# Attention scores computed once per head in 64x32 array tiles, with an expert loop that turns each block's rows at its own start

## The chip, the cores and the metric

The kernel runs on one core of a Trainium2 chip. A core has TensorE (matrix products, written PE in profiles, with its weight loads as PEld), VectorE (DVE), ScalarE (ACT), GpSimd (POOL) and SyncE (SP), which here only issues transfers. Each engine works through its own instructions in order and waits for others through semaphores. The metric is the device time of one execution in microseconds (us); all data are 32-bit floats.

## The reference

There are B = 8 batches of H = 8 heads. Each head has 512 rows of x and 32 rows of state, of width 64. The first half is an attention in both directions, the second a mixture of 8 experts in which a token either takes the expert of its own largest logit or keeps that of the token before.

```python
scores = scale * x @ state.T              # (512, 32) per head
a = softmax(scores, over the 32)          # x reads from the state
xread = a @ state
scores2 = scale * state @ x.T             # (32, 512): the same numbers, turned
a2 = softmax(scores2, over the 512)       # the state reads from x
sread = a2 @ x
x = concat([xread, sread], rows)          # per batch 544 tokens of 8*64 = 512

logits = x @ w_gate                       # 8 per token
local_gate = sigmoid(x @ w_local)
e = argmax(logits) if first token or local_gate < 0.5 else expert of the token before
out = softmax(logits)[e] * (relu(x @ w1[e]) @ w2[e])     # 512 -> 1024 -> 512
```

## The kernel before

The program has three stages, one after another: `attention` (L90), `Routing.route` (L282) and `experts` (L395). In all of them a scheduler decides the order in which each engine gets its instructions, from the order of the code and from the dependencies; on the engine the order is then fixed.

**Attention** goes through the 8 batches. The heads of a batch are held as two groups of four (g), each group as two 128-partition slices (k) of two heads. `std` (L105 to L111) holds the state of each head spread with zeros, so that a product over 128 partitions keeps heads apart. `weights(b, g)` (L134) makes the scores twice: `s2` (L139) with the state rows on the partitions and 512 tokens along the row, and `s1` (L145) with tokens on the partitions. From s2 comes the softmax over tokens, `e2` (L149 to L162), and from s1 the one over the 32 state rows, `e1` (L156 to L167; the last multiplication is on GpSimd). `turned` (L170) turns both with TensorE against an identity, e2 at L174 and e1 at L179, and copies them out of PSUM with ScalarE (L176) and VectorE (L181). `read(b)` (L184) makes the state's reading of x (L189), and for each of four chunks of 128 tokens the values (L202, 256 columns for each group) and, with the same weights, the logits (L205, 9 columns: eight experts and the local gate). For the latter, `sw` (state times gate weights, L117 to L125) is made once ahead of the loop. The values leave PSUM at L208, the state's rows are turned at L215 and their logits made at L218. Then the softmax of the logits (L223 to L233) is appended to each row, and rows go to DRAM (L234, L235) as 520 numbers: 512 values and 8 probabilities. The loop (L240) runs `turned` of batch b, the scores of b+1 and `read` of b.

**Routing** finds each token's expert, sorts tokens into blocks of 128 that share an expert, and writes for each block the tokens to gather (`gidx`), the places to scatter to (`sidx`), the expert (`bei`, `ohb`) and the number of blocks in use (`nbi`, L339). 4352 tokens fill between 34 and 41 blocks.

**Experts** runs over the blocks. `gather(k)` (L407) fetches 128 rows by an indirect transfer of GpSimd into one of four buffers. `load(k)` (L413) reads the expert's number into a register of SyncE and loads its two weight matrices, 2 MB each, into one of two buffers each. `turn(k)` (L423) turns the rows with four TensorE transposes (L427), copies them out with VectorE (L429), and picks the probability `p` of the block's expert (L430, L431). `block(k)` (L438) does the first product in two halves (L447) with the relu on ScalarE (L449), then the second product (L458), the scaling by p on VectorE (`y`, L460) and the scatter by GpSimd (L461). Between the two products of block k stand `load(k + 1)`, `turn(k + 1)` and `gather(k + 3)` (L451 to L455). The first 34 blocks run always, the last 7 each under a condition that holds only while blocks are left:

```python
    n = nc.values_load(nbi[0:1, 0:1], min_val=NJ, max_val=NBLK, ...)
    for k in range(NJ):
        block(k)
    with ExitStack() as held:
        for k in range(NJ, NBLK):
            held.enter_context(tc.If(n > k))
            block(k)
```

PSUM is one pool of 8 banks (`bank`, L64) for all stages.

Of the kernel before, what the change touches and what calls it, by code (L numbers as in the profile page):

```python
# [17 lines left out]
P = 128  # L18
# [12 lines left out]
XW = D + E  # L31
# [7 lines left out]
def kernel(  # L39
# [18 lines left out]

    nc = tc.nc
    keep = ctx.enter_context(tc.tile_pool(name="keep", bufs=1))  # L60
    ps = ctx.enter_context(tc.tile_pool(name="ps", bufs=8, space=PSUM))
    dram = ctx.enter_context(tc.tile_pool(name="dram", bufs=1, space=DRAM))

    def bank(parts=P):  # L64
        return ps.tile([parts, 512], F32, tag="ps", name="ps")
# [8 lines left out]
    nbi = keep.tile([1, 1], I32, name="nbi")  # L74
# [7 lines left out]
    route = Routing(ctx, tc, bank, ident)  # L82
    with ExitStack() as phase:
        attention(phase, tc, bank, xn, xt, st, stt, ident, wg, lt, mx, rows)
    route.route(lt, mx, gidx, sidx, ohb, bei, nbi)
    with ExitStack() as phase:
        experts(phase, tc, bank, w1, w2, ident, rows, gidx, sidx, ohb, bei, nbi, out)


def attention(ctx, tc, bank, xn, xt, st, stt, ident, wg, lt, mx, rows):  # L90
# [3 lines left out]
    wk = ctx.enter_context(tc.tile_pool(name="wk", bufs=4))  # L94
    tp = ctx.enter_context(tc.tile_pool(name="tp", bufs=4))
    rp = ctx.enter_context(tc.tile_pool(name="rp", bufs=2))
    sm = ctx.enter_context(tc.tile_pool(name="sm", bufs=4))


    stc = once.tile([P, B, G, DH], F32, name="stc")  # L100
    nc.scalar.dma_start(out=stc.rearrange("p b g d -> p (b g d)"), in_=st)
    sttc = once.tile([P, B, KT, N], F32, name="sttc")
    nc.sync.dma_start(out=sttc.rearrange("p b k n -> p (b k n)"), in_=stt)
    sd = once.tile([P, B, G, GD], F32, name="sd")
    std = once.tile([P, B, KT, P], F32, name="std")  # L105
    nc.vector.memset(std, 0.0)
    nc.gpsimd.memset(sd, 0.0)
    for m in range(2):
        for u in range(2):
            r, c = slice(64 * u, 64 * u + 64), slice(64 * m + 32 * u, 64 * m + 32 * u + 32)  # L110
            nc.vector.tensor_copy(std[r, :, m::2, c], sttc[r, :, m::2, :])  # L111
    for j in range(4):
        r = slice(32 * j, 32 * j + 32)
        nc.scalar.copy(sd[r, :, :, 64 * j:64 * j + 64], stc[r])


    wps = bank()  # L117
    for b in range(B):
        for g in range(G):
            i = (b * G + g) * (E + 1)  # L120
            for k in (2 * g, 2 * g + 1):
                nc.tensor.matmul(wps[:, i:i + E + 1], lhsT=std[:, b, k, :], rhs=wg[:, k, :],  # L122
                                 start=(k == 2 * g), stop=(k == 2 * g + 1))
    sw = once.tile([P, B, G, E + 1], F32, name="sw")
    nc.scalar.copy(sw.rearrange("p b g e -> p (b g e)"), wps[:, :B * G * (E + 1)])  # L125
# [8 lines left out]
    def weights(b, g, x_t):  # L134


        s2 = bank()
        for k in (2 * g, 2 * g + 1):
            nc.tensor.matmul(s2, lhsT=std[:, b, k, :], rhs=x_t[:, k, :],  # L139
                             start=(k == 2 * g), stop=(k == 2 * g + 1))  # L140

        s1 = bank()
        for c in range(SC):
            for k in (2 * g, 2 * g + 1):
                nc.tensor.matmul(s1[:, c * P:c * P + P], lhsT=x_t[:, k, c * P:c * P + P],  # L145
                                 rhs=std[:, b, k, :], start=(k == 2 * g), stop=(k == 2 * g + 1))

        nb = sm.tile([P, 1], F32, name="nb")
        nc.vector.tensor_reduce(nb, s2, axis=AX, op=Alu.max)  # L149
        nc.vector.tensor_scalar(nb, nb, -SCALE, None, Alu.mult)  # L150
        e2 = wk.tile([P, S], F32, name="e2")
        z2 = sm.tile([P, 1], F32, name="z2")
        nc.scalar.activation(e2, s2, Act.Exp, bias=nb, scale=SCALE, accum_out=z2)
        m1 = sm.tile([P, SC * 4, 1], F32, name="m1")
        s1v = s1.rearrange("p (a n) -> p a n", n=N)
        nc.vector.tensor_reduce(m1.rearrange("p a o -> p (a o)"), s1v, axis=AX, op=Alu.max)  # L156
        e1 = wk.tile([P, SC * 4, N], F32, name="e1")
        nc.vector.tensor_tensor(e1, s1v, m1.to_broadcast([P, SC * 4, N]), op=Alu.subtract)
        nc.scalar.activation(e1, e1, Act.Exp, scale=SCALE)
        nc.vector.tensor_scalar(z2, z2, 1e-9, None, Alu.add)  # L160
        nc.vector.reciprocal(z2, z2)  # L161
        nc.vector.tensor_scalar(e2, e2, z2, None, Alu.mult)  # L162
        z1 = sm.tile([P, SC * 4, 1], F32, name="z1")
        nc.vector.tensor_reduce(z1.rearrange("p a o -> p (a o)"), e1, axis=AX, op=Alu.add)
        nc.vector.tensor_scalar(z1, z1, 1e-9, None, Alu.add)
        nc.vector.reciprocal(z1, z1)
        nc.gpsimd.tensor_tensor(e1, e1, z1.to_broadcast([P, SC * 4, N]), op=Alu.mult)  # L167
        return e1.rearrange("p a n -> p (a n)"), e2

    def turned(e1, e2):  # L170

        t2 = bank()
        for c in range(SC):
            nc.tensor.transpose(t2[:, c * P:c * P + P], e2[:, c * P:c * P + P], ident)  # L174
        e = tp.tile([P, SC, P], F32, name="e")
        nc.scalar.copy(e.rearrange("p c n -> p (c n)"), t2)  # L176
        t1 = bank()
        for c in range(SC):
# [324 lines left out]
```

## Time and profile before

| what | value |
|---|---|
| time, median of 3 runs (lowest to highest) | 784.79 us (783.58 to 785.57) |
| the profiled execution's own time | 784.79 us |
| its span, first to last instruction | 783.0 us |
| TensorE busy | 739.7 us (94%) |
| VectorE / ScalarE / GpSimd busy | 185.4 / 107.5 / 100.6 us |
| mean granted TensorE clock | 0.962 |
| moved by DMA | 211.03 MB, mean 270 GB/s |
| attention, to the last product L218 | 178.0 us |
| routing, to the first L447 | 178.0 to 221.2 us |
| experts, to the last y | 221.2 to 772.6 us |
| from there to the end of the span | 10.4 us |

A profile shows one execution. A group of instructions is shown as line, engine, operation, the tiles written and read, shapes and a count, then busy time in us, the mean duration of one in ns, and the idle time of that engine just before with what ended it. The chain of waits follows the last instruction back to what released it, step by step. A matmul's recorded end is a modelled one, so durations of neighbouring matmuls overlap; starts are what can be subtracted. A product of 32-bit floats is recorded as two matmuls, each with its own weight load; a transpose as one. Idle time of an engine that nobody waits for costs nothing.

### The profile page before, as it was taken

How to read it: one execution, taken by the hardware profiler on the slowest of the kernel's cores; microseconds unless marked ns; L12 is line 12 of the kernel's file. 1: busy time of each engine (PE TensorE's matmuls, PEld its weight loads, DVE VectorE, ACT ScalarE, POOL GpSimd, SP SyncE). 2: the span in 40 equal slices, each digit the busy share in tenths (PEclk: the TensorE clock that was granted, in tenths of full speed). 3: DMA queues.
4: the chain of work that ended last, by engine and by line, in shares of the span. 5: the costliest groups of instructions: out<-in, count | busy, mean ns of one | idle time of the engine just before them, and what ended most of it. 6: DMA issues, size and time to landing. Idle time of an engine off the chain costs nothing.

```text
span 783.0 us, 10576 instructions
## 1 busy us (share of the span) xinstructions
PE 739.7 (94%) x4410; PEld 568.0 (73%) x4410; DVE 185.4 (24%) x517; ACT 107.5 (14%) x194; POOL 100.6 (13%) x107
## 2 busy tenths in 40 slices
PE   6799999992879999999999999999999999999994
PEld 6588888891867867767767768778678677677682
DVE  3455555537611011101101111110110111011010
ACT  0433333330000000100100000000001001000000
POOL 2111111110031111111111111111111111111120
PEclk9899999996579999999999999999999999999997
DMA  8134553112948888898888888888888989888881
GB/s 368 62 108 166 186 189 128 59 59 75 412 125 321 343 322 317 332 338 319 325 344 307 319 338 333 315 327 338 311 318 340 328 316 336 334 295 311 333 319 63
DMA packets 24946, 211.03 MB, mean 270 GB/s; under 512 B 3456, under 2 KB 3456, under 8 KB 12864
## 3 DMA queue, kind: packets, MB, share of 16 engines
q1 hardware_dynamic: 13824, 180.90, 62.5%
q0 software_dynamic: 6320, 19.84, 6.5%
q10 hardware_dynamic: 4752, 9.58, 3.3%
q8 instruction: 37, 0.61, 0.3%
q14 instruction: 13, 0.11, 0.0%
HBM read 192.34 MB, written 19.01 MB: 270 GB/s over the span
## 4 chain that ended last, share of the span: by engine, by line
PE 92%; DVE 3%; DMA 2%; issue 1%; POOL 0%; SPq 0%; POOLq 0%; DVEq 0%
PE ps L447 34%; PE ps L458 32%; PE ps L139 4%; PE ps L202 4%; PE ps L145 4%; PE ps L189 4%; PE ps L388 2%; PE ps L427 2%; PE ps L122 2%; PE ps L205 1%; DMA out_dram<-y,sidx 1%; PE ps L179 1%; PE ps L174 1%; DMA sttc<-in_stt_dram 1%; PE ps L215 0%
## 5 line engine op out<-in xcount | busy, mean ns | idle before, releaser
L447 PEld LDWEIGHTS ps<-x_t,a 128*128 128x128 f32 x2432 | 279.5, 193 | 18.9 <-issue 17.7
L447 PE MATMUL ps<-x_t,a 128*128 128x128 f32 x2432 | 279.8, 276 | 0.8 <-DVE x_t L429 0.8
L458 PE MATMUL ps<-c,h 128*128 128x512 f32 x608 | 267.2, 592 | 0.0
L458 PEld LDWEIGHTS ps<-c,h 128*128 128x128 f32 x608 | 112.6, 190 | 127.2 <-issue 127.2
L449 ACT ACTIVATE h<-ps 128x512 f32<-128x512 f32 x76 | 45.4, 597 | 541.6 <-PE ps L447 541.6
L429 DVE COPY x_t<-ps 128x512 f32<-128x512 f32 x39 | 27.0, 692 | 246.6 <-PE ps L427 246.6
L460 DVE TENSOR_SCALAR y<-ps,p 128x512 f32<-128x512 f32 x38 | 28.5, 751 | 234.8 <-PE ps L458 234.8
L461 POOL DMA_INDIRECT out_dram<-y,sidx x38 | 38.4, 1011 | 289.5 <-DVE p L431 263.9
L409 POOL DMA_INDIRECT xg<-rows,gidx x41 | 40.2, 980 | 242.6 <-PE ps L427 188.4
L145 PEld LDWEIGHTS ps<-std,x_t 128*128 128x128 f32 x256 | 31.4, 193 | 8.5 <-issue 8.5
L202 PE MATMUL ps<-sd,a 128*128 128x256 f32 x128 | 35.3, 398 | 0.0
L167 POOL TENSOR_TENSOR e<-e,z 128x512 f32<-128x512 f32 x16 | 16.8, 1048 | 141.3 <-DVE z L161 108.9
L139 PE MATMUL ps<-x_t,std 128*128 128x512 f32 x64 | 33.4, 649 | 0.0
L145 PE MATMUL ps<-std,x_t 128*128 128x128 f32 x256 | 31.2, 275 | 0.0
L189 PE MATMUL ps<-e,x_n 128*128 128x64 f32 x256 | 29.5, 273 | 0.0
L189 PEld LDWEIGHTS ps<-e,x_n 128*128 128x128 f32 x256 | 29.2, 192 | 0.0
L427 PE MATMUL ps<-ident,xg 128*128 128x128 f32 x156 | 23.9, 277 | 4.1 <-DMA xg<-rows,gidx 4.1
L388 PE MATMUL ps<-bc,pc 128*128 128x41 f32 x80 | 17.3, 415 | 9.9 <-DVE bc L383 9.9
L388 PEld LDWEIGHTS ps<-bc,pc 128*128 128x128 f32 x80 | 17.1, 332 | 10.8 <-issue 10.8
L208 ACT COPY xr<-ps 128x512 f32<-128x512 f32 x32 | 18.8, 586 | 36.6 <-PE ps L202 36.6
L202 PEld LDWEIGHTS ps<-sd,a 128*128 128x128 f32 x128 | 21.9, 191 | 1.6
L427 PEld LDWEIGHTS ps<-ident,xg 128*128 128x128 f32 x156 | 18.6, 143 | 4.3 <-issue 4.3
(125 smaller groups left out, 326.4 us busy)
## 6 DMA issues: line engine op xcount, KB each, us to landing
a<-in_w_dram SPq DMA_DIRECT2D x39, 2048.0 KB, 8.4
c<-in_w_dram SPq DMA_DIRECT2D x39, 2048.0 KB
rows<-xr ACTq DMA_DIRECT2D x8, 1040.0 KB, 4.4
x_t<-in_xt_dram SPq DMA_DIRECT2D x8, 1024.0 KB, 8.7
x_n<-in_xn_dram SPq DMA_DIRECT2D x8, 1024.0 KB, 5.1
xg<-rows,gidx POOLq DMA_INDIRECT x41, 7.9
out_dram<-y,sidx POOLq DMA_INDIRECT x38, 6.9
rows<-xs ACTq DMA_DIRECT2D x8, 65.0 KB, 4.0
```

The lines of the kernel that those rows point to most:

```text
L139: nc.tensor.matmul(s2, lhsT=std[:, b, k, :], rhs=x_t[:, k, :], start=(k == 2 * g), stop=(k == 2 * g + 1))
L145: nc.tensor.matmul(s1[:, c * P:c * P + P], lhsT=x_t[:, k, c * P:c * P + P], rhs=std[:, b, k, :], start=(k == 2 * g), stop=(k == 2 * g + 1))
L189: nc.tensor.matmul(rps[:, k, :], lhsT=x_n[:, c, 2 * k:2 * k + 2, :].rearrange("p h d -> p (h d)"), rhs=e_t[k // 2][:, c, 64 * (k % 2):64 * ...
L202: nc.tensor.matmul(v[:, g * GD:g * GD + GD], lhsT=a_t[g][:, c * P:c * P + P], rhs=sd[:, b, g, :], start=True, stop=True)
L388: nc.tensor.matmul(who, lhsT=pc, rhs=bc[:, c], start=(c == 0), stop=(c == COLS - 1))
L409: nc.gpsimd.indirect_dma_start(out=xg, out_offset=None, in_=rows[:, :], in_offset=bass.IndirectOffsetOnAxis(ap=gidx[:, k:k + 1], axis=0))
L427: nc.tensor.transpose(tps[:, j * P:j * P + P], xg[:, j * P:j * P + P], ident)
L447: nc.tensor.matmul(hps[:, i * P:i * P + P], lhsT=a[:, j, m * P:m * P + P], rhs=x_t[:, j, :], start=(j == 0), stop=(j == KT - 1))
L449: nc.scalar.activation(h[:, half * 4:half * 4 + 4, :].rearrange("p m t -> p (m t)"), hps, Act.Relu)
L458: nc.tensor.matmul(yps, lhsT=h[:, m, :], rhs=c[:, m, :], start=(m == 0), stop=(m == FK - 1))
L460: nc.vector.tensor_scalar(y, yps, p, None, Alu.mult)
L461: nc.gpsimd.indirect_dma_start(out=out, out_offset=bass.IndirectOffsetOnAxis(ap=sidx[:, k:k + 1], axis=0), in_=y, in_offset=None, bounds_c ...
```

## The change

The attention is written anew, and the expert loop has another form.

Scores are made once. `sttc`, the state with two heads on the partitions (64 each), is used as it is: for each of the four slices k and two halves u, one product over 64 partitions gives 32 rows, so that the eight products of a batch address eight different 64x32 tiles of the array. They fill a tile of two PSUM banks, `s`. The softmax over tokens works on s as before (e2). For the one over the state's rows, VectorE turns s in 32x32 squares into `e1`; the maximum, the difference (now GpSimd), the exponential, the sum and the quotient follow, and a second 32x32 transpose gives `a`, which then needs no turn on TensorE. The operations on e1 cover both groups, 1024 elements in a row. `gates` puts the state times the gate weights beside the spread state in `sd`, so that one value product of 265 columns gives values and a part of the logits; the parts of the two groups are added (L206). Rows in DRAM have 530 numbers. PSUM is split: two banks in a pool for attention, two for s, four for values; eight for routing and experts, which share a pool opened later. Work buffers of attention have two copies in place of four.

In the experts, buffers come from pools: two copies of the weights, three of the gathered rows. Block k begins with its load, the gather of k+2, p, the four transposes and their copy, and then has its two products, y and the scatter. The conditions and `nbi` are gone: all 41 blocks run. The order of the rows of w1 is changed ahead of the launch to fit the new order of heads.

The core of the diff:

```diff
-XW = D + E
+VW = GD + E + 1
+XW = G * VW
...
+    def scores(b, x_t):
+        s = sps.tile([P, G, S], F32, name="s")
+        for k in range(KT):
+            for u in range(G):
+                r = slice(64 * u, 64 * u + 64)
+                nc.tensor.matmul(s[32 * k:32 * k + 32, u, :], lhsT=sttc[r, b, k, :], rhs=x_t[r, k, :],
+                                 start=True, stop=True)
+        return s
+
+    def gates():
+        for u in range(G):
+            w = bank()
+            r = slice(64 * u, 64 * u + 64)
+            for b in range(B):
+                for k in range(KT):
+                    nc.tensor.matmul(w[32 * k:32 * k + 32, b * (E + 1):(b + 1) * (E + 1)],
+                                     lhsT=sttc[r, b, k, :], rhs=wg[r, k, :], start=True, stop=True)
+            nc.vector.tensor_copy(sd[:, :, u, GD:], w[:, :B * (E + 1)].rearrange("p (b e) -> p b e", b=B))
...
-        nc.vector.tensor_tensor(e1, s1v, m1.to_broadcast([P, SC * 4, N]), op=Alu.subtract)
-        nc.scalar.activation(e1, e1, Act.Exp, scale=SCALE)
+        e1 = wk.tile([P, G * SC * 4, N], F32, name="e1")
+        e1f = e1.rearrange("p a n -> p (a n)")
+        nc.vector.transpose(e1f, s.rearrange("p g s -> p (g s)"))
...
+        nc.vector.tensor_reduce(m1.rearrange("p a o -> p (a o)"), e1, axis=AX, op=Alu.max)
+        nc.gpsimd.tensor_tensor(e1, e1, m1.to_broadcast([P, G * SC * 4, N]), op=Alu.subtract)
+        nc.scalar.activation(e1f, e1f, Act.Exp, scale=SCALE)
...
-        nc.gpsimd.tensor_tensor(e1, e1, z1.to_broadcast([P, SC * 4, N]), op=Alu.mult)
+        nc.gpsimd.tensor_tensor(e1, e1, z1.to_broadcast([P, G * SC * 4, N]), op=Alu.mult)
+        a = tp.tile([P, G, S], F32, name="a")
+        nc.vector.transpose(a.rearrange("p g s -> p (g s)"), e1f)
...
-        t1 = bank()
-        for c in range(SC):
-            nc.tensor.transpose(t1[:, c * P:c * P + P], e1[:, c * P:c * P + P], ident)
-        a = tp.tile([P, S], F32, name="a")
-        nc.vector.tensor_copy(a, t1)
...
         for c in range(SC):
-            v = bank()
-            for g in range(G):
-                nc.tensor.matmul(v[:, g * GD:g * GD + GD], lhsT=a_t[g][:, c * P:c * P + P],
-                                 rhs=sd[:, b, g, :], start=True, stop=True)
-            for g in range(G):
-                nc.tensor.matmul(lps[:, c * (E + 1):(c + 1) * (E + 1)],
-                                 lhsT=a_t[g][:, c * P:c * P + P], rhs=sw[:, b, g, :],
-                                 start=(g == 0), stop=(g == G - 1))
-            nc.scalar.copy(xr[:, c, :D], v)
+            v = vps.tile([P, G, 512], F32, name="v")
+            for u in range(G):
+                nc.tensor.matmul(v[:, u, :VW], lhsT=a[:, u, c * P:c * P + P], rhs=sd[:, b, u, :],
+                                 start=True, stop=True)
+            nc.scalar.copy(xr[:, c], v[:, :, :VW])
+        nc.vector.tensor_tensor(lt[:, :SC, b, :], xr[:, :, 0, GD:], xr[:, :, 1, GD:], op=Alu.add)
...
     for b in range(B):
-        at = [turned(*s) for s in soft.pop(b)]
+        e = turned(soft[1])
+        a = soft[0]
...
         if b + 1 < B:
-            soft[b + 1] = [weights(b + 1, g, xs_[b + 1][0]) for g in range(G)]
+            soft = softmaxes(scores(b + 1, xs_[b + 1][0]))
...
-    def turn(k, xg):
+    xgs = {k: gather(k) for k in range(2)}
+    for k in range(NBLK):
+        a, c = load(k)
+        if k + 2 < NBLK:
+            xgs[k + 2] = gather(k + 2)
+        xg = xgs.pop(k)
+        own = gp.tile([P, E], F32, name="own")
+        nc.vector.tensor_tensor(own, xg[:, GD:GD + E], ohb[:, k], op=Alu.mult)
+        p = gp.tile([P, 1], F32, name="p")
+        nc.vector.tensor_reduce(p, own, axis=AX, op=Alu.add)
         tps = bank()
         for j in range(KT):
...
+            nc.tensor.transpose(tps[:, j * P:j * P + P], xg[:, at:at + P], ident)
+        x_t = hp.tile([P, KT, P], F32, name="x_t")
         nc.vector.tensor_copy(x_t.rearrange("p k t -> p (k t)"), tps)
...
-        if k + 1 < NBLK:
-            ws[k + 1] = load(k + 1)
-            ready[k + 1] = turn(k + 1, xgs.pop(k + 1))
-        if k + 3 < NBLK:
-            xgs[k + 3] = gather(k + 3)
         yps = bank()
...
-    for k in range(NJ):
-        block(k)
-    with ExitStack() as held:
-        for k in range(NJ, NBLK):
-            held.enter_context(tc.If(n > k))
-            block(k)
```

In the changed file the score products are L131, the gate products L141, the 32x32 transposes L153 and L173, the turns of e2 L181, the value products L203, the state's rows L212 and L215; in the experts own is L425, p L427, the transposes L431, their copy L433, the first product L440, the second L445, y L447 and the scatter L448.

## The prediction

> **What bounds the kernel now.** I read the stages first, because the page's mean over the span hides that the program is three different programs. The view of busy time by stage (columns: engine busy us with the number of instructions; the granted TensorE clock; DMA share and rate) gives:
>
> ```profile
> core 0: us, PE busy (x) PEld busy (x) DVE busy (x) ACT busy (x) POOL busy (x), PEclk, DMA share, GB/s
> 64.90:168.50 103.60, 103.60 (x756) 90.00 (x754) 57.97 (x185) 39.94 (x79) 12.59 (x12) 1.00 0.36 127
> 178.00:221.00 43.00, 22.25 (x98) 19.91 (x98) 28.70 (x94) 0.48 (x2) 4.04 (x5) 0.54 0.61 236
> 221.00:772.60 551.60, 551.36 (x3192) 405.61 (x3192) 66.31 (x152) 45.38 (x76) 73.52 (x74) 1.00 0.86 317
> ```
>
> The reader sees TensorE busy without a hole in attention (103.60 of 103.60 us) and in the experts (551.36 of 551.60), and neither in the routing stage between (22.25 of 43.00), which is a chain of small VectorE steps and 40 short products. So a TensorE microsecond removed from attention, or added to the experts, moves the end one for one until another engine becomes late.
>
> The costs of attention are in the groups by form (each product in the code is two recorded matmuls: 32 products at L139, 64 records). A record's mean ns includes its modelled tail, so I take start-to-start times from the timeline where I can:
>
> ```profile
> L139 PE MATMUL ps<-x_t,std 128*128 128x512 f32 x64 | 33.4, 649 | 0.0
> L145 PE MATMUL ps<-std,x_t 128*128 128x128 f32 x256 | 31.2, 275 | 0.0
> L179 PE MATMUL ps<-ident,e 128*128 128x128 f32 x64 | 10.2, 285 | 2.1 <-POOL e L167 2.1
> L205 PE MATMUL ps<-sw,a 128*128 128x9 f32 x128 | 16.3, 236 | 0.0
> L149 DVE TENSOR_REDUCE nb<-ps 128x1 f32<-128x512 f32 x16 | 11.1, 691 | 24.2 <-PE ps L139 24.2
> L167 POOL TENSOR_TENSOR e<-e,z 128x512 f32<-128x512 f32 x16 | 16.8, 1048 | 141.3 <-DVE z L161 108.9 <-PE ps L202 16.4 <-DVE z L166 16.0
> ```
>
> The handover between two expert blocks is in the timeline. Columns: start, duration, engine, line:
>
> ```profile
> 432.78 0.60 PE L427 MATMUL ps<-ident,xg 128*128 128x128 f32 x4
> ...
> 433.21 7.03 PE L458 MATMUL ps<-c,h 128*128 128x512 f32 x16
> 433.41 0.69 DVE L429 COPY x_t<-ps 128x512 f32<-128x512 f32 x1 [6.43 <-PE ps L427]
> ...
> 440.08 6.19 PE L447 MATMUL ps<-x_t,a 128*128 128x128 f32 x54
> 440.28 0.33 SPq L419 DMA_DIRECT2D c<-in_w_dram  x1
> 440.29 0.75 DVE L460 TENSOR_SCALAR y<-ps,p 128x512 f32<-128x512 f32 x1 [6.18 <-PE ps L458]
> ```
>
> The turning of the next block (L427, 0.43 us from its start to the next stream's) stands between the two products of this block, its copy (L429) lies under L458, and L447 of the next block follows L458 at once. Period 14.45 us: 7.15 for L447, 0.43, 6.87 for L458. And the program runs fewer blocks than it holds:
>
> ```profile
> L409 POOL DMA_INDIRECT xg<-rows,gidx x41 | 40.2, 980 | 242.6 <-PE ps L427 188.4 <-DVE gone L391 51.8 <-issue 1.8
> L461 POOL DMA_INDIRECT out_dram<-y,sidx x38 | 38.4, 1011 | 289.5 <-DVE p L431 263.9 <-DVE own L430 13.5 <-DVEq L469 12.2
> ```
>
> 41 gathers but 38 scatters: with this data the conditions (L471) end the loop after 38 of 41 blocks. From the first L447 at 221.23 to the last y at 772.63 are 551.4 us = 38 x 14.45 + 2.3 (a first block at a low clock).
>
> [...] L158, 512 elements, shows 691 ns[...]; so 1024 elements are estimated at 1.22 us. [...] the trace's clock is 1.00 in the experts, so I keep full clock there.
>
> **The change, part by part.** The profiled execution took 784.79 us, span 783.0, and is also the median of the three runs; sums are made against it. It divides into attention to 178.0, routing to 221.2 (43.2), experts 551.4 and a tail of 10.4.
>
> *Expert handover.* In the changed program's order TensorE has L431 (four transposes) right before L440 of the same block, after L445 of the block before. VectorE has y of the block before (L447 there) and right behind it the copy x_t (L433). Let T0 be when the array comes free. Transposes are done by T0+0.43. From the timeline, y starts at T0+0.21 (440.29 against 440.08) and lasts 0.75; back-to-back VectorE instructions start about 0.08 before the former's recorded end (758.18+0.75 against 758.85), so x_t runs from T0+0.88 to T0+1.57; TensorE starts 0.05 later (as at 221.23, behind the copy that ended at 221.18). That is T0+1.62, and 0.10 for a weight load that is no longer hidden: 1.72 where it was 0.43. Period 7.15+6.87+1.72 = 15.74, +1.29. Ends: 1.55 (load hidden, copy overlapping more) and 1.90 (the whole 0.19 us load and slower restarts). Nothing covers it: the array has no other work in its order. Below zero is excluded because the copy stands ahead of the first product in the data flow.
>
> *Three more blocks.* No condition is left, so 41 blocks run; the last three scatter nothing but load weights and multiply. From first L440 to last y: 40 x 15.74 + 14.02 + 2.3 = 645.9, against 551.4: **+94.5** (three blocks about 47, the handovers about 47). The removed conditions and the block count give nothing back: the period is 14.45 before and after block 34. Weight loads keep two buffers and the same releases; 4.2 MB per 15.74 us is a lower rate than now. Of the moved steps: VectorE has own(k+3) ahead of y(k), and it waits for gather k+3, so y and x_t queue behind that gather. It is issued about 1 us into block k and landings here are at most 9.0 us, some 5 us early: cost 0. Without that cover each late microsecond would cost one per block. On POOL gather k+4 stands ahead of scatter k, both at the block's start, 1 us each; y has two buffers and a scatter lands in 6.9: 0.
>
> *Attention on TensorE.* Gone per batch (period 18.42): L139 3.44, L145 3.57, the e1 transposes L179 0.86, L205 1.40 (4 x 0.35): 9.3. Kept: e2 transposes 0.86, L189 3.52, the value products 0.96 per chunk times 265/256 for their 9 extra columns, x 4 = 3.96, L215 and L218 0.88: 9.22. New: 8 score products, each two records of 512 columns at 0.43. Bounds: all tiles at once 0.9[...], one after another 16 x 0.43 = 6.9. I take 9 x 0.43 = 3.9: the second record of a product needs the same tile as the first[...]. So TensorE has 13.1 per batch (10.1 to 16.1).
>
> *Attention on the others, per batch.* VectorE: five passes over 1024 elements (two maxima, one sum, two 32x32 transposes) 6.1; two e2 scalings 1.0; small softmax steps 0.9; rt 0.58; logits 0.36; routing statistics 1.3: 10.2, against 10.3 now (57.97 in 5.63 batches). POOL: two 1024-element operations, 2 x 2.1. ACT about 7.2. So TensorE still leads; a transpose of fp32 at a quarter of the estimated rate would add 7.3 and make VectorE the bound at 17.5. The chain from scores to a (1.22+0.15+1.22+1.22+2.1+1.06+1.22+0.44+2.1+1.22 = 12.0) is hidden in steady state, since scores stand up to two batches ahead of their value products. It shows once, at the start.
>
> *Attention's end.* The gate products: 64, so 128 records; with 32-column weights L218 takes 0.044 each warm, at twice that cold: 5.6 to 11.3, say 8.5, from 5.5 (the state's landing) to 14. First scores to 19. The chain with 1.5 of queueing: first value product at 32.5. Left on TensorE: 8 x (3.96+0.88) + 7 x (0.86+3.52) + 6 x 3.9 = 92.8. With 5 us for waits: **130, against 178: -48**. At the ends: all tiles at once, then VectorE leads: 32 + 7.5 x 10.2 + 4 = 113; in series 32.5 + 110.8 + 9 = 152.
>
> *Routing, tail.* The same instructions but one; 43.4, since the last lt now follows an ACT copy. Tail 10.
>
> Sum: 130 + 43.4 + 645.9 + 10 = 829.3, against 783.0: +46, so **831** for the 784.8.
>
> **Rivals.** *(a) Scores in series or a slow transpose:* the tiles don't overlap. For: two records per product[...]. Attention ends at 152: 853. This is also the case where the change doesn't do what it says. *(b) Attention better:* scores fully side by side, VectorE leads at 10.2: ends at 113, 814. *(c) Handover hidden:* the expert stage keeps 14.45 because TensorE gets its x_t without idling; then 41 x 14.45 + 2.3 = 594.8 is only +43, and attention's -48 leaves 780, faster. It decides once the handover is below about 0.57 (40 x (h-0.43) + 43 = 48). For it: VectorE is busy only 66 of 551 us. Against: the order puts y's 0.75 and the copy's 0.69 in series with TensorE. *(d) The gather ahead of y lands late:* 2 us a block, 910; landings of 9.0 at most speak against it.
>
> **How the numbers follow.** Main case 62% (range 822 to 842); (a) 17%; (b) 15%; (c) 4%; (d) 2%. The range for 8 in 10 takes (a) and (b) in and leaves out their far parts, with 40 x 0.18 = 7 for the handover's bounds partly inside: 812 to 853. About 0.3% is what a measurement of this kernel can tell from no change. Slower 0.95; (c) gives most of faster 0.04; between 0.01.
>
> **What would show it.** 41 scatters; block starts 15.7 apart; TensorE idle about 1.3 a block, ended by the x_t copy; x_t directly behind y. In attention, score records spanning about 3.9 per batch, a period near 13, transposes near 1.2 us, the routing stage starting near 130. Wrong if transposes take several us, if score records stand one behind another, or if own's wait for a gather ends the idle time before y.

## The result, and the profile after

The changed kernel takes 835.23 us (median of 4 runs, 834.05 to 836.63), the kernel before 784.18 in the same comparison (4 runs). The ratio is 1.065, with a 95% interval of 1.0626 to 1.0673: slower by 6.5%. The profiled execution took 836.63 us, its span is 834.8.

The view of busy time by stage, for the changed kernel (29 us is where its first value product starts, 136 where its last one ends, 179.9 where its first expert product starts; columns as before):

```profile
core 0: us, PE busy (x) PEld busy (x) DVE busy (x) ACT busy (x) POOL busy (x), PEclk, DMA share, GB/s
29.00:128.50 99.50, 86.81 (x544) 62.94 (x545) 68.55 (x152) 44.91 (x88) 25.95 (x20) 0.89 0.45 164
128.50:136.00 7.50, 7.50 (x55) 6.51 (x53) 1.64 (x8) 1.79 (x4) 0.00 (x0) 0.92 0.42 155
136.00:179.80 43.80, 22.34 (x99) 19.93 (x98) 28.77 (x94) 0.84 (x2) 3.52 (x4) 0.55 0.60 234
179.80:825.30 645.50, 605.09 (x3440) 436.39 (x3440) 63.50 (x162) 48.97 (x82) 77.26 (x78) 1.00 0.77 284
```

In the experts TensorE was busy in 551.36 of 551.60 us; now it is in 605.09 of 645.50, so 40 us of holes are new. They hold 41 blocks instead of 38. In attention, TensorE was busy without a hole at clock 1.00; now it has 12.7 us of holes in 99.5 us (and none in the 7.5 after them), and the mean clock is 0.89. The routing stage is what it was.

The bill by stage, of the two profiled executions: attention ends at 136.0 instead of 178.0 (-42.0), routing takes 43.9 instead of 43.2 (+0.7), the experts from first product to last y take 645.4 instead of 551.4 (+94.0), the tail 9.5 instead of 10.4 (-0.9). The sum is +51.8, which is the difference of the spans, 834.8 and 783.0.

The groups by form show the new operations and the block count (out<-in, shape, count; busy us, mean ns; idle time before, with its releasers):

```profile
L440 PE MATMUL ps<-x_t,a 128*128 128x128 f32 x2624 | 306.0, 278 | 41.0 <-DVE x_t L433 40.2 <-issue 0.8
L448 POOL DMA_INDIRECT out_dram<-y,sidx x41 | 41.7, 1016 | 69.2 <-DVE y L447 58.0 <-issue 11.3
L131 PE MATMUL s<-x_t,sttc 64*32 64x512 f32 x128 | 20.6, 715 | 9.2 <-ACT e L157 7.2 <-DMA x_t<-in_xt_dram 2.0
L173 DVE STREAM_TRANSPOSE a<-e 128x1024 f32<-128x1024 f32 x8 | 9.9, 1244 | 6.9 <-POOL e L171 6.9
L153 DVE STREAM_TRANSPOSE e<-s 128x1024 f32<-128x1024 f32 x8 | 9.9, 1238 | 0.0
L224 DVE TENSOR_TENSOR pr<-lt,mx 128x40 f32<-128x40 f32 x8 | 7.6, 952 | 0.2
L163 DVE TENSOR_SCALAR z<-z 128x2 f32<-128x2 f32 x8 | 4.0, 494 | 1.3 <-ACT e L157 1.3
L141 PE MATMUL ps<-wg,sttc 64*32 64x9 f32 x128 | 1.8, 199 | 4.3 <-DMA sttc<-in_stt_dram 4.3
```

L440 names the cause of the expert holes: 40.2 us of idle time ended by the copy x_t, 1.00 us for each of 40 handovers. L448 counts 41 scatters where before had 38. A 32x32 transpose of 1024 elements takes 1.24 us, from PSUM (L153) and from SBUF (L173) alike. L224 is the surprise: an operation on 40 elements with a mean of 952 ns. The same step (L226 there) was 200 ns in the kernel before.

One handover, in the timeline of the changed kernel (start, duration, engine, line):

```profile
431.97 0.60 PE L431 MATMUL ps<-ident,xg 128*128 128x128 f32 x4
...
432.17 0.75 DVE L447 TENSOR_SCALAR y<-ps,p 128x512 f32<-128x512 f32 x1 [6.79 <-PE ps L445]
432.84 0.68 DVE L433 COPY x_t<-ps 128x512 f32<-128x512 f32 x1
...
433.57 7.41 PE L440 MATMUL ps<-x_t,a 128*128 128x128 f32 x64 [1.00 <-DVE x_t L433]
...
440.80 0.17 DVE L425 TENSOR_TENSOR own<-xg,ohb 128x8 f32<-128x8 f32 x1 [7.22 <-DMA xg<-rows,gidx]
...
440.82 5.75 PE L445 MATMUL ps<-c,h 128*128 128x512 f32 x13
```

Transposes at 431.97; y occupies VectorE first, from 432.17; the copy comes behind it, at 432.84; the first product starts at 433.57, 1.60 us after the transposes. From there to L445 are 7.25 us, 0.10 more than the 7.15 of before: the first weight load starts together with the first product, where before it lay 0.43 us ahead, under L458. 1.60 + 7.25 + 6.87 = 15.72 is the period; it was 14.45.

### What attention waits for

In three places, holes of TensorE in attention are followed by a stretch at half its clock. TensorE's timeline of the changed kernel at the first of them:

```profile
49.93 0.66 PE L181 MATMUL ps<-ident,e 128*128 128x128 f32 x4
53.94 6.47 PE L190 MATMUL ps<-e,x_n 128*128 128x64 f32 x32 [3.35 <-ACT e L182]
60.20 5.23 PE L203 MATMUL v<-sd,a 128*128 128x265 f32 x12
```

and the windows around it (the number after the busy times is the granted clock):

```profile
core 0: us, PE busy (x) PEld busy (x) DVE busy (x) ACT busy (x) POOL busy (x), PEclk, DMA share, GB/s
52.00:56.00 4.00, 2.06 (x13) 2.06 (x13) 3.11 (x9) 2.16 (x6) 1.91 (x1) 0.83 0.58 236
56.00:60.00 4.00, 4.00 (x21) 4.00 (x20) 1.78 (x5) 0.00 (x0) 1.91 (x1) 0.50 0.00 0
60.00:64.00 4.00, 4.00 (x11) 3.15 (x12) 1.76 (x8) 1.21 (x2) 0.00 (x0) 0.50 0.61 205
```

There are 3.35 us of idle time, then 10.2 us at 0.50 (54.7 to 64.9): L190 takes 6.47 us for the 32 records that take 3.78 at full clock (at 100.91 in the same trace), and the 12 records of L203 5.23 where late_dve, below, has 2.97. So 5 us are lost behind a stall of 3.35. The clock is also 0.50 from 78.6 to 85.4, around the end of the gap that ends at 79.9, and from 122.9 to 129.8, after several gaps from 119 on. Smaller holes, 0.73 us ahead of 29.02 and 0.88 ahead of 36.47, leave it at 1.00. Which length of idle time brings the half clock is not shown here: it came behind a gap of 3.35 us, within one of 4.05, and, in the section below on what was not expected, behind one of 0.92.

Two waits make up most of the 12.7 us: 4.1 us for the copies of the turned e2 (L182; 3.35 of them up to 53.94) and 4.8 us for the transposes of e1 (L173; 4.05 of them up to 79.91).

What made TensorE wait at 50? The second of two ScalarE copies (L182). ScalarE's timeline, same kernel:

```profile
49.03 0.59 ACT L182 COPY e<-ps 128x512 f32<-128x512 f32 x1 [1.27 <-PE ps L181]
53.18 0.24 ACT L225 ACTIVATE pr<-pr 128x40 f32<-128x40 f32 x1 [3.56 <-DVE pr L224]
53.32 0.57 ACT L182 COPY e<-ps 128x512 f32<-128x512 f32 x1
```

The exponential of the logits (L225, 40 elements, of the batch before) stands in ScalarE's order between the two copies, and waits 3.56 us for VectorE's L224. VectorE has meanwhile:

```profile
50.09 1.22 DVE L148 TENSOR_REDUCE nb<-s 128x2 f32<-128x1024 f32 x1 [2.46 <-PE s L131]
51.23 1.21 DVE L168 TENSOR_REDUCE z<-e 128x32 f32<-128x1024 f32 x1
...
53.01 0.14 DVE L224 TENSOR_TENSOR pr<-lt,mx 128x40 f32<-128x40 f32 x1
```

Two reductions over 1024 elements stand ahead of L224. So a step on 40 elements, whose result only goes into the rows to be stored, holds up the next batch's reading of the state.

At other places L224 itself is long. VectorE and GpSimd in the changed kernel's timeline:

```profile
73.70 1.91 POOL L161 TENSOR_TENSOR e<-e,m 128x1024 f32<-128x1024 f32 x1 [4.76 <-DVE z L169]
...
74.12 1.55 DVE L224 TENSOR_TENSOR pr<-lt,mx 128x40 f32<-128x40 f32 x1
...
75.57 1.91 POOL L171 TENSOR_TENSOR e<-e,z 128x1024 f32<-128x1024 f32 x1
75.59 1.91 DVE L163 TENSOR_SCALAR z<-z 128x2 f32<-128x2 f32 x1
```

L224 (40 elements) ends at 75.67, when GpSimd's L161 ends at 75.61; L163 (2 elements) ends at 77.50, GpSimd's L171 at 77.48. The reader sees an operation of VectorE held for the whole of one of GpSimd. Behind these two stands the other long wait of TensorE: GpSimd takes up the quotient L171 only after L161 of the other batch, and on VectorE the transpose L173 comes behind the held L163 and five short steps, from 78.61 to 79.85; TensorE then starts at 79.91, after 4.05 us without work. The whole trace has the same: the four of the eight L224 that meet a GpSimd pass take 1.55 to 1.91 us, the other four 0.14 to 0.20. The reductions that meet one are not held: L222 takes 0.14 to 0.20 us in three such places, and L160 1.21 us in the one at 25.56, as elsewhere. What makes this difference is not shown.

### The profile page after: what moved, and what is told of

The parts are those of the page before. It is cut to its first block, busy times and chain, and to the rows that moved or that the text cites. A ratio compares the mean times of both kernels' runs of the same rounds, so it can differ in the third digit from the quotient of the medians.

```text
span 834.8 us, 10290 instructions
## 1 busy us (share of the span) xinstructions
PE 736.5 (88%) x4338; PEld 534.0 (64%) x4338; DVE 177.2 (21%) x442; ACT 102.9 (12%) x187; POOL 122.5 (15%) x122
## 4 chain that ended last, share of the span: by engine, by line
issue 68%; PE 10%; DVE 8%; POOL 7%; DMA 4%; ACT 1%; POOLq 0%; SPq 0%; ACTq 0%
POOL out_dram L448 4%; DMA out_dram<-y,sidx 3%; PE v L203 3%; PE ps L388 2%; POOL xg L403 2%; PE s L131 2%; PE ps L190 2%; DVE nb L148 1%; DVE pr L224 1%; DVE e L153 1%; DMA x_t<-in_xt_dram 1%; PE ps L181 1%; DVE z L168 1%; DVE a L173 1%; DVE m L160 1%
## 5 line engine op out<-in xcount | busy, mean ns | idle before, releaser
L440 PE MATMUL ps<-x_t,a 128*128 128x128 f32 x2624 | 306.0, 278 | 41.0 <-DVE x_t L433 40.2
L440 PEld LDWEIGHTS ps<-x_t,a 128*128 128x128 f32 x2624 | 298.2, 193 | 50.9 <-DVE x_t L433 49.7
L445 PE MATMUL ps<-c,h 128*128 128x512 f32 x656 | 288.3, 592 | 0.0
L445 PEld LDWEIGHTS ps<-c,h 128*128 128x128 f32 x656 | 121.5, 190 | 137.3 <-issue 137.3
L447 DVE TENSOR_SCALAR y<-ps,p 128x512 f32<-128x512 f32 x41 | 30.8, 751 | 296.2 <-PE ps L445 296.2
L425 DVE TENSOR_TENSOR own<-xg,ohb 128x8 f32<-128x8 f32 x41 | 6.9, 167 | 289.2 <-DMA xg<-rows,gidx 289.2
L448 POOL DMA_INDIRECT out_dram<-y,sidx x41 | 41.7, 1016 | 69.2 <-DVE y L447 58.0
L203 PE MATMUL v<-sd,a 128*128 128x265 f32 x128 | 40.6, 461 | 6.0 <-DVE a L173 4.8
L190 PEld LDWEIGHTS ps<-e,x_n 128*128 128x128 f32 x256 | 33.3, 212 | 7.0 <-ACT e L182 5.0
L203 PEld LDWEIGHTS v<-sd,a 128*128 128x128 f32 x128 | 26.8, 224 | 17.2 <-DVE a L173 6.6
L190 PE MATMUL ps<-e,x_n 128*128 128x64 f32 x256 | 33.7, 296 | 4.1 <-ACT e L182 4.1
L431 PEld LDWEIGHTS ps<-ident,xg 128*128 128x128 f32 x164 | 20.7, 143 | 25.4 <-issue 21.1
L431 PE MATMUL ps<-ident,xg 128*128 128x128 f32 x164 | 25.1, 277 | 4.1 <-DMA xg<-rows,gidx 4.1
L131 PE MATMUL s<-x_t,sttc 64*32 64x512 f32 x128 | 20.6, 715 | 9.2 <-ACT e L157 7.2
L433 DVE COPY x_t<-ps 128x512 f32<-128x512 f32 x41 | 27.9, 681 | 0.8 <-PE ps L431 0.8
L388 PEld LDWEIGHTS ps<-bc,pc 128*128 128x128 f32 x80 | 17.1, 332 | 10.8 <-DVE bc L383 10.8
L205 ACT COPY xr<-v 128x530 f32<-128x530 f32 x32 | 18.8, 599 | 31.8 <-PE v L203 30.4
L161 POOL TENSOR_TENSOR e<-e,m 128x1024 f32<-128x1024 f32 x8 | 15.3, 1913 | 31.4 <-DVE m L160 18.7
L171 POOL TENSOR_TENSOR e<-e,z 128x1024 f32<-128x1024 f32 x8 | 15.3, 1912 | 30.7 <-DVE z L170 20.7
```

The costliest lines, as they stand in the source:

```text
L131: nc.tensor.matmul(s[32 * k:32 * k + 32, u, :], lhsT=sttc[r, b, k, :], rhs=x_t[r, k, :], start=True, stop=True)
L190: nc.tensor.matmul(rps[:, k], lhsT=x_n[:, c, 2 * k:2 * k + 2, :].rearrange("p h d -> p (h d)"), rhs=e[:, c, :, 32 * k:32 * k + 32], start= ...
L203: nc.tensor.matmul(v[:, u, :VW], lhsT=a[:, u, c * P:c * P + P], rhs=sd[:, b, u, :], start=True, stop=True)
L388: nc.tensor.matmul(who, lhsT=pc, rhs=bc[:, c], start=(c == 0), stop=(c == COLS - 1))
L431: nc.tensor.transpose(tps[:, j * P:j * P + P], xg[:, at:at + P], ident)
L433: nc.vector.tensor_copy(x_t.rearrange("p k t -> p (k t)"), tps)
```

## The experiments

The first five take the change apart, col_one tests the scores, and the others look for what holds attention.

**exp_old: the new attention with the old expert loop** (attention, routing and row layout of the changed kernel, `experts` of the kernel before, which reads the new layout)

```diff
-            nc.tensor.transpose(tps[:, j * P:j * P + P], xg[:, j * P:j * P + P], ident)
+            at = (j // 2) * VW + (j % 2) * P
+            nc.tensor.transpose(tps[:, j * P:j * P + P], xg[:, at:at + P], ident)
-        nc.vector.tensor_tensor(own, xg[:, D:], ohb[:, k], op=Alu.mult)
+        nc.vector.tensor_tensor(own, xg[:, GD:GD + E], ohb[:, k], op=Alu.mult)
```

> The new attention with the expert loop of before (turn ahead, conditions, fixed buffers). Theory (the change is a sum of independent parts: attention -42, handovers +51, three more blocks +47): attention ends at 136, then 43.8 routing, 38 blocks of 14.45, in all about 743 us. Rival (the stages touch: rows of 530 numbers and the denser loop cost more, or the gain of attention is given back later): 755 or more, with a period above 14.45.

Measured: 742.94 us, ratio to before 0.9494 (0.9461 to 0.9527). The new attention alone makes the kernel faster by 41 us.

**attn_old: the old attention with the new expert loop** (attention and row layout of the kernel before, `experts` of the changed one, reading the old layout)

```diff
-            at = (j // 2) * VW + (j % 2) * P
-            nc.tensor.transpose(tps[:, j * P:j * P + P], xg[:, at:at + P], ident)
+            nc.tensor.transpose(tps[:, j * P:j * P + P], xg[:, j * P:j * P + P], ident)
```

> The attention of before with the new expert loop. Theory (sum of parts): 178.0 + 43.2 + 645.4 + 9.6, about 877 us, period 15.72. Rival (the new loop's stall comes from the new layout of rows and probabilities): a period nearer to 14.45, about 830 us.

Measured: 877.78 us, 1.1189 (1.1167 to 1.1211). The period of a block is 15.72 us as in the changed kernel. The new expert loop alone costs 94 us. The parts add up: -41.2 + 93.6 = +52.4 against +51 for the whole change (835.2 less 784.2), so they hardly act on each other.

**ahead41: the changed kernel with the turn back between the two products, still 41 blocks**

```diff
+    def turn(k):
         xg = xgs.pop(k)
...
         nc.vector.tensor_copy(x_t.rearrange("p k t -> p (k t)"), tps)
+        return x_t, p
+
+    ready = {0: turn(0)}
...
+        x_t, p = ready.pop(k)
         h = hp.tile([P, FK, P], F32, name="h")
...
+        if k + 1 < NBLK:
+            ready[k + 1] = turn(k + 1)
         yps = bank()
```

> The changed kernel with only the turning of the next block moved back between the two products; 41 blocks and pools stay. Theory (the handover is y, then the copy, in front of the first product): period 14.45, 40 x 1.27 = 51 less, 784 us. Rival (VectorE's own, ahead of y, waits for a late gather, or the pools of two hold the loop): period stays near 15.7, 835 us.

Measured: 786.03 us, 1.0017 (1.0005 to 1.0029). Its timeline has the order of the kernel before:

```profile
435.89 0.60 PE L427 MATMUL ps<-ident,xg 128*128 128x128 f32 x4
...
436.33 7.03 PE L452 MATMUL ps<-c,h 128*128 128x512 f32 x16
436.53 0.69 DVE L429 COPY x_t<-ps 128x512 f32<-128x512 f32 x1 [5.67 <-PE ps L427]
...
443.20 6.97 PE L445 MATMUL ps<-x_t,a 128*128 128x128 f32 x61
```

The copy lies under the second product, and the next first product follows that one at once: a period of 14.45. The place of the turn alone is worth 835.2 - 786.0 = 49 us, 40 handovers of 1.2.

**start38: the turn at the block's start, but with the conditions, so 38 blocks** (on exp_old)

```diff
-    ready = {0: turn(0, xgs.pop(0))}
...
-        x_t, p = ready.pop(k)
+        x_t, p = turn(k, xgs.pop(k))
...
-            ready[k + 1] = turn(k + 1, xgs.pop(k + 1))
```

> The new attention; the expert loop with the conditions and fixed buffers of before, but with each block turned at its own start, so 38 blocks run. Theory: period 15.72, three blocks less, 835 - 47 = 788 us. Rival (conditions cost time that the new loop saved): each of the four conditional blocks that run longer by 1 us or more, 792 us and above.

Measured: 790.64 us, 1.009 (1.0069 to 1.011), with the new period of 15.72. Against the changed kernel the three blocks are worth 835.2 - 790.6 = 45 us, or 14.9 each. The figure lies nearer to the first expectation, and is 2.6 us above it. The trace shows what the conditions add: from one y to the next are 15.72 us, but 16.07 into the first conditional block and 15.99 into each of the other three, 1.2 us in all and not the rival's 4. In exp_old, with the turn ahead, these blocks keep 14.45. The other 1.4 us stay open; the runs of the two kernels spread over 1.7 and 2.6 us.

**copy_act: the x_t copy on ScalarE**

```diff
-        nc.vector.tensor_copy(x_t.rearrange("p k t -> p (k t)"), tps)
+        nc.scalar.copy(x_t.rearrange("p k t -> p (k t)"), tps)
```

> The changed kernel with the copy of the turned rows on ScalarE, so that it no longer stands behind y on VectorE; all else as changed, 41 blocks. Theory (y's 0.75 us stands in front of the copy): transposes 0.43, 0.20 to the copy, 0.59 for it, 0.15 to the first product: handover 1.37, period 15.39, 13 us less than 835, about 822. Rival (the handover is set by restarting TensorE or by a gather): period stays at 15.72, 835 us.

Measured: 824.98 us, 1.0513 (1.0486 to 1.054); 10.2 us less than the changed kernel. Its timeline:

```profile
440.76 0.60 PE L431 MATMUL ps<-ident,xg 128*128 128x128 f32 x4
...
440.96 0.75 DVE L447 TENSOR_SCALAR y<-ps,p 128x512 f32<-128x512 f32 x1 [5.99 <-PE ps L445]
441.45 0.58 ACT L433 COPY x_t<-ps 128x512 f32<-128x512 f32 x1 [6.76 <-PE ps L431]
...
442.09 7.41 PE L440 MATMUL ps<-x_t,a 128*128 128x128 f32 x64 [0.73 <-ACT x_t L433]
```

The copy no longer waits for y, and runs beside it. The handover falls from 1.60 to 1.33 us, no further, as transposes, copy and start stay in series: 40 times 0.27 are 10.8. Another engine for the copy recovers a fifth of the 49 us; another place in the order recovers all.

**col_one: all score products in one column tile** (on exp_old; s is made once, ahead of the loop, and filled with zeros)

```diff
-                nc.tensor.matmul(s[32 * k:32 * k + 32, u, :], lhsT=sttc[r, b, k, :], ...)
+                nc.tensor.matmul(s[0:32, u, :], lhsT=sttc[r, b, k, :], ...)
```

> The new attention with the expert loop of before (743 us), with the four score products of each half addressed to one and the same column tile: it leaves out three of four heads of each half, whose scores are zero. Theory (products run side by side only in different tiles): the score records of a batch span 8 x 0.43 = 3.4 us where they span 1.0 now, and since TensorE idles some 15% in this stage, the time rises by 8 to 19, to 751 to 762 us. Rival (the tile makes no difference): span 1.0, 743 us.

Measured: 766.93 us, 0.9746 (0.9703 to 0.9789): 24 us more than exp_old, somewhat over what was expected. Its timeline:

```profile
61.55 3.94 PE L134 MATMUL s<-x_t,sttc 64*32 64x512 f32 x12
...
65.55 1.23 DVE L151 TENSOR_REDUCE nb<-s 128x2 f32<-128x1024 f32 x1 [1.22 <-PE s L134]
```

12 records of a batch now take 3.94 us, and VectorE's maximum waits for the last. In the changed kernel all 16 take 1.09. The first row has all of them, the second those still running at 75.6:

```profile
74.77 1.09 PE L131 MATMUL s<-x_t,sttc 64*32 64x512 f32 x16
```
```profile
75.22 0.64 PE L131 MATMUL s<-x_t,sttc 64*32 64x512 f32 x8
```

Eight records start within 0.05 us at 74.77, the other eight within 0.05 us at 75.22. One after another, at the 0.43 us that a record of 512 columns takes elsewhere (16 of L445 in 6.87), sixteen would take 6.9, so the eight tiles run side by side, and a second round of eight records follows the first. Which record of which product is in which round is not told by the rows. A smaller group costs no less. Another batch of the changed kernel has its scores in two groups, one product and then seven:

```profile
66.14 1.04 PE L131 MATMUL s<-x_t,sttc 64*32 64x512 f32 x2
67.11 0.66 PE L181 MATMUL ps<-ident,e 128*128 128x128 f32 x4
67.70 1.08 PE L131 MATMUL s<-x_t,sttc 64*32 64x512 f32 x14
68.71 1.16 PE L203 MATMUL v<-sd,a 128*128 128x265 f32 x4
```

By the starts, the one product holds TensorE for 0.97 us and the seven for 1.01. The order on TensorE cuts the scores of the last six batches into 14 groups of 2 to 16 records, each 0.97 to 1.09 us, 13 of them after 29.0. So a batch's scores cost 2.3 us on average and not 1.0.

**bufs4: four copies of the work tiles instead of two** (on exp_old)

```diff
-    wk = ctx.enter_context(tc.tile_pool(name="wk", bufs=2))
-    tp = ctx.enter_context(tc.tile_pool(name="tp", bufs=2))
+    wk = ctx.enter_context(tc.tile_pool(name="wk", bufs=4))
+    tp = ctx.enter_context(tc.tile_pool(name="tp", bufs=4))
```

> The new attention with the expert loop of before (743 us), four copies of the softmax and turned tiles in place of two. Theory C (the halved buffers keep batches from overlapping): at least 5 less, 738 us or below. Theories A and B (the engines' own order and VectorE with GpSimd set the pace): 741 to 745 us.

Measured: 743.48 us, 0.947 (0.9445 to 0.9494), no different from exp_old. These buffers are not what attention waits for. The smaller pools of PSUM were not varied; TensorE's waits that end with a copy out of PSUM (L181 behind L219, L203 behind L205) are 2.5 us of the 12.7 in the changed kernel.

**dve_e1: the two e1 passes of GpSimd on VectorE** (on exp_old)

```diff
-        nc.gpsimd.tensor_tensor(e1, e1, m1.to_broadcast([P, G * SC * 4, N]), op=Alu.subtract)
+        nc.vector.tensor_tensor(e1, e1, m1.to_broadcast([P, G * SC * 4, N]), op=Alu.subtract)
...
-        nc.gpsimd.tensor_tensor(e1, e1, z1.to_broadcast([P, G * SC * 4, N]), op=Alu.mult)
+        nc.vector.tensor_tensor(e1, e1, z1.to_broadcast([P, G * SC * 4, N]), op=Alu.mult)
```

> The new attention with the expert loop of before (743 us), the difference and the quotient of e1 moved from GpSimd to VectorE. Theory A (GpSimd's 1.91 us operations hold small VectorE operations up and lengthen the chain): the operations of up to 1.9 us at the logits' difference fall to 0.2, VectorE gains 1.3 and pays 2.4 per batch, and the chain is 1.4 shorter: 731 to 739 us. Theory B (VectorE sets the pace): 7 x 2.4 = 17 more, 755 to 760 us.

Measured: 738.06 us, 0.9402 (0.9379 to 0.9425), 4.9 us less than exp_old, though VectorE has two passes of 1.22 us more per batch. The groups by form of this kernel:

```profile
L225 DVE TENSOR_TENSOR pr<-lt,mx 128x40 f32<-128x40 f32 x8 | 1.3, 168 | 0.0
L164 DVE TENSOR_SCALAR z<-z 128x2 f32<-128x2 f32 x8 | 1.2, 148 | 0.2 <-ACT e L158 0.2
```

These are L224 and L163 of the changed kernel: 168 ns where it had 952, 148 where it had 494. With GpSimd's passes gone the holding is gone, so GpSimd was what held them. Holes are left: TensorE idles 3.26 us up to 77.99, again for the second copy of the turned e2 (L183 in this file), which on ScalarE now stands behind an exponential (L158) that has waited 2.07 us for VectorE. The clock is 0.50 from 80 to 88; it falls once more, to 0.72, from 120 to 124.

**late: the softmax of the logits one batch later** (on exp_old)

```diff
-        read(b, a, e, xs_.pop(b)[1])
+        done = read(b, a, e, xs_.pop(b)[1])
+        if b > 0:
+            finish(*last)
+        last = done
+    finish(*last)
```

(`finish` is the end of `read`, from the maximum of the logits on; the pool of xr and xs has three copies instead of two.)

> The new attention with the expert loop of before (743 us), the softmax of each batch's logits taken one batch later and three copies of the rows, so that on ScalarE the copies of the turned e2 no longer stand behind the logits' exponential. Theory D (engine queues: TensorE waits for those copies, and each wait of some 4 us also halves its clock for about 10 us after): no slice of attention at clock 0.5, attention 8 to 15 shorter, 728 to 735 us. Theory A alone (GpSimd's hold on VectorE and the chain's length): no change, 741 to 745 us.

Measured: 739.58 us, 0.9408 (0.9372 to 0.9443), 3.4 us less than exp_old: neither of the figures expected. The stall has moved. TensorE's timeline of this kernel:

```profile
54.88 1.58 PE L204 MATMUL v<-sd,a 128*128 128x265 f32 x4 [2.53 <-DVE a L174]
56.25 6.93 PE L191 MATMUL ps<-e,x_n 128*128 128x64 f32 x32
```

TensorE's wait for the copies falls to 1.9 us, from 4.1 in exp_old; now the value products wait 2.53 us for the last transpose of e1 (a, 53.59 to 54.82). It follows GpSimd's quotient (51.41 to 53.32) and, on VectorE, a maximum of the next scores. The clock is again 0.50 from 56 to 64, and L191 takes 6.93 us. One stall was removed and the next in line took its place. Over the stage the clock is better (0.95 from the first value product to the end of attention, against 0.87 in exp_old), but TensorE still idles 9.6 us (9.3), and its first value product starts at 32.0 instead of 28.8. With the later softmax some small operations are also longer: L164 and L234 have means of 772 and 900 ns, where exp_old has 493 and 304 (its L164 and L231).

**late_dve: both edits together** (on late)

```diff
-        nc.gpsimd.tensor_tensor(e1, e1, m1.to_broadcast([P, G * SC * 4, N]), op=Alu.subtract)
+        nc.vector.tensor_tensor(e1, e1, m1.to_broadcast([P, G * SC * 4, N]), op=Alu.subtract)
...
-        nc.gpsimd.tensor_tensor(e1, e1, z1.to_broadcast([P, G * SC * 4, N]), op=Alu.mult)
+        nc.vector.tensor_tensor(e1, e1, z1.to_broadcast([P, G * SC * 4, N]), op=Alu.mult)
```

> As before, with the later softmax of the logits and the difference and quotient of e1 on VectorE as well. If queue order (D) and GpSimd's hold (A) are separate costs, the gains add: 722 to 731 us, with all of attention at full clock. If they are one and the same wait, no better than the better of the two alone, 733 to 738 us; if VectorE becomes the bound (11.5 us of work per batch), 738 us or above.

Measured: 723.3 us, 0.9198 (0.9151 to 0.9246), the fastest of all here, 8% under the kernel before. The two edits save 4.9 and 3.4 us alone, and 19.6 together. The window over the middle of attention, and TensorE's timeline:

```profile
core 0: us, PE busy (x) PEld busy (x) DVE busy (x) ACT busy (x) POOL busy (x), PEclk, DMA share, GB/s
36.00:104.00 68.00, 66.97 (x486) 49.07 (x485) 64.34 (x150) 36.40 (x77) 0.52 (x5) 1.00 0.54 195
```
```profile
45.98 3.79 PE L191 MATMUL ps<-e,x_n 128*128 128x64 f32 x32
...
57.57 3.79 PE L191 MATMUL ps<-e,x_n 128*128 128x64 f32 x32
```

TensorE is busy in 66.97 of 68 us at clock 1.00, and a batch takes 11.59 us. This is TensorE's own work: by the starts, 1.99 us for two groups of scores and 9.6 for the other products. VectorE is busy in 64.34 of 68: it is nearly as full, with the two passes that it took over. The routing stage's first scan starts at 119.2 instead of 141.4 in the changed kernel. The full clock holds up to 105, but not to the end of attention: it is 0.50 from 105.3 to 112.1. The two edits together give more than twice the sum of what each gives alone. The traces agree with a simple reason: each edit alone leaves stalls of the other cause. From the first value product to the end of attention TensorE idles 9.6 us in late, 11.4 in dve_e1, and 1.0 with both.

## Why the prediction was right, and where its terms were off

The prediction was 831 us, 812 to 853, slower; the median is 835.23. Step by step:

- **The handover** was right in each of its parts. Predicted were y at +0.21, the copy from +0.88 to +1.57, start at +1.62, and 0.10 for the load: 1.72, period 15.74. Measured were +0.20, +0.87 to +1.55, +1.60, and 0.10: period 15.72. ahead41 shows that the place of the turn is the cause (period 14.45), copy_act that y's place ahead of the copy is 0.27 of it.
- **Three more blocks** were right: 41 scatters, and 645.4 us from first product to last y where 645.9 was predicted. start38 puts the three blocks at 45 us (predicted about 47), ahead41 the 40 handovers at 49 (40 x 1.29 = 52). The low clock of the first block is in both traces: 0.50 up to 225.3 in the kernel before and up to 184.4 in the changed one.
- **Covers named in that step** held: own waits for its gather in every block (7.22 us up to 440.80, in which VectorE has nothing else to do), and is through some 7 us ahead of y. The clock stays at 1.00 in the experts in spite of a 1.00 us hole per block.
- **Attention's end** was predicted at 130, -48, and measured at 136.0, -42. Behind that small miss stand larger ones of opposite sign:
  - *Scores*, "I take 9 x 0.43 = 3.9" per batch, was the author's estimate, since no product of before uses such a tile; it put most of the 16 records one behind another. In a lone product (66.14) the second record does start 0.45 us after the first, but in a group it does not hold up the other tiles: eight records start together, and the lower bound of 0.9, all tiles at once, was near (1.0 to 1.1 for a group). What neither bound had is that a batch's scores come in one to three groups of about 1 us each. 13 groups, 13.0 us, followed after 29.0, where 6 x 3.9 = 23.4 was counted: 10.4 too much. col_one shows how a real queue on one column would have looked: 24 us.
  - *The start.* The gate products, "say 8.5", measured 1.8 us, 0.014 a record. (The "cold" factor of two in that sum shows in the trace of before, by the starts: four records of L139 take 3.29 us from 21.04 and 1.72 from 26.12.) The first scores end at 10.1 instead of 19. The chain from there took 18.9 us instead of 13.5; among its steps on VectorE stand some of the next batch (L148 at 22.93, L153 at 24.15). So the first value product starts at 29.0 instead of 32.5.
  - *Waits*, "With 5 us for waits". With 92.8 - 10.4 = 82.4 us left on TensorE at 29.0, it would have ended at 111.4. It ended at 136.0, so 24.6 us are waits and half clock, and the 5 was the largest miss. The trace separates the two: 12.7 us are idle time, and in the three stretches at clock 0.50 TensorE is busy for 21.8 us (10.24, 5.47 and 6.13), of which about 10.9 are lost; 1.0 is left over. The 10.9 is an estimate, which takes work at half clock to last twice as long; the L190 at 53.94 agrees, with 6.26 us to the next row, 5.54 of them at half clock, against 3.62 at full.
- **The false step behind that term** is that the chain from scores to a "is hidden in steady state". "So TensorE still leads" held, though by less than was thought. VectorE's work per batch was sized well (10.2, measured 10.4 with the held time in it; GpSimd's pass 1.91 for 2.1). The 1.22 for 1024 elements, transposes among them, was an estimate; before's operations on 8 and on 512 elements (L430 165 ns, L158 691), continued in a straight line, give 1.23, and measured were 1.20 to 1.22 for the reductions and 1.24 for the transposes. TensorE's is 11.6 in late_dve (busy 66.97 us of 68). With two engines so nearly full, an order that puts small steps in the way soon makes TensorE wait. Nor did the prediction count what GpSimd's longer passes do to VectorE's small operations. dve_e1, late and late_dve show both causes: with both removed, attention runs at 11.59 us per batch and full clock up to 105.
- **Rivals.** (b), scores side by side, had the mechanism of the scores right; its 113 for attention's end was missed by the stalls. late_dve comes near it, its last state logits (L216) start at 114, but not for the reason given: there TensorE leads at 11.59 a batch, not VectorE at 10.2. (a) is excluded by the records. (c), the handover hidden, is what ahead41 is: 786.0, near the 780 that this rival was given. (The handover at which it would decide comes out of its own sum at 0.55 to 0.56, not 0.57.) (d) did not happen.
- **Routing and tail**: predicted 43.4 and 10, measured 43.9 and 9.5.

So the sign and the expert stage were predicted by their mechanism. The total owes part of its nearness to chance: 10.4 us too much for scores and 3.5 at the start, against 19.6 too little for waits.

## What to carry to other kernels

A step that moves from under a long product to the head of the next one costs its whole chain (transposes, what stands ahead on the copying engine, the copy, the restart), once per block, here 1.27 us; read that chain from the timeline, it can be had to 0.02 us. When a change makes the leading engine lighter, look again for who is then nearly as full: small operations in an in-order queue, which cost nothing before, become stalls, and here the half clock behind one TensorE stall of 3.35 us cost another 5. When one edit against such stalls shows little, try it together with the next before dropping it: here two edits worth 4.9 and 3.4 us alone were worth 19.6. And look at how the order cuts up products that are meant to run side by side, since each group here cost as much as all of them together (0.97 to 1.09 us).

## What was not expected of the hardware

- Eight fp32 products of 64 rows by 32 columns, in eight tiles of the array, take 1.09 us with both records of each (16 records of 512 columns); one such product alone holds TensorE for 0.97 us. 64 products of 9 columns take 1.8 us.
- Two small operations of VectorE, L224 (40 elements) and L163 (2 elements), were held to the end of a GpSimd pass of 1.91 us where they started within it: both took up to 1.91 us in place of 0.14 to 0.2.
- The granted clock was not told by the last gap alone. In the experts a hole of 1.00 us per block leaves it at 1.00. In late_dve a gap of 0.92 us ahead of 102.94 is followed by clock 0.82 from 104 to 106 and 0.50 from 106 to 112, with TensorE busy all that time. In late TensorE is busy for only 2.16 and 2.56 of 4 us from 116 to 124, and the clock stays at 1.00. What else sets it stays open. The three stretches at 0.50 within the changed kernel's attention last 10.24, 6.83 and 6.83 us; those in exp_old, dve_e1, late and late_dve, worked out from the mean clock of 2 or 4 us slices, 3.4, 6.8 or 10.2.
